# Two more units transposed by DMA, w_out conversions moved out of the last chunk, and a blockwise end

## The chip, the cores and the metric

The kernel runs on one core of one Trainium2 chip. The metric is the time of one execution on the device in microseconds (us); where several runs are given, their median. A core has five engines with a queue of instructions each: TensorE (PE; its weight loads are shown apart as PEld), VectorE (DVE), ScalarE (ACT), GpSimd (POOL) and SyncE (SP). SyncE only issues transfers here; 16 DMA engines carry them out. TensorE writes only to PSUM, whose contents VectorE or ScalarE have to take out ("evict") before the bank can be used again.

## The reference

A recurrent retention layer is followed by a feed-forward layer with SiLU. Cut to what matters:

```python
# q, k, v: (batch 4, heads 8, seq 768, head_dim 64), float32
gamma = 1.0 - 2.0 ** (-5.0 - np.arange(H, dtype=np.float32))
for t in range(S):
    state = gamma[None, :, None, None] * state + np.einsum('bhd,bhe->bhde', k[:, :, t], v[:, :, t])
    y[:, :, t] = scale * np.einsum('bhd,bhde->bhe', q[:, :, t], state)

x = y.transpose(0, 2, 1, 3).reshape(B * S, H * D)      # (3072, 512)
h = x @ w_in                                           # w_in (512, 2048)
g = h * (1.0 / (1.0 + np.exp(-h)))
out = g @ w_out                                        # w_out (2048, 512)
```

The two weights arrive as 64-bit floats (two 32-bit words per number), and the result is float32.

## The kernel before

The sequence is cut into 6 chunks of 128 positions. A unit is one chunk of one batch entry, so there are 24 units, numbered 0 to 23, four to a chunk. For each unit a "visit" m does three things for three neighbouring units: it prepares unit m, computes the scores and states of unit m - 1, and the output y of unit m - 2. Between the visits stand the products x @ w_in: 16 slices f of each chunk c, each of twelve 128x512 matmuls. Every float32 operand is split into a high and a low part and a mixed third one, so that one product is three matmuls: two add up in `ha` (or `oa`), one in `hb` (or `ob`), and an eviction combines the two. The results g go to DRAM and come back for the last part, g @ w_out.

A unit needs k and q with the head dimension on the partitions. Up to unit 16 TensorE transposes them (`stage_t`), from unit 17 on the DMA does: GpSimd pulls the 32-bit numbers apart into two 16-bit planes, the DMA transposes the planes, ScalarE puts them together.

```python
    FAR = 4 * B + 1                  # B = 4: from unit 17 on by DMA

    def part_t(n):
        for name, (p, tag, bufs) in (("q", (ld, "kf", 3)), ("k", (one, "kt", 2))):
            src = kqv[name].pop(n) if name == "q" else kqv[name][n]
            t = p.tile([128, 2 * H * D], U16, tag=tag, name=f"{name}p_{n}", bufs=bufs)
            nc.gpsimd.tensor_copy(out=t.rearrange("p (w h d) -> p w h d", w=2, h=H),
                                  in_=src.bitcast(U16).rearrange("p h (d w) -> p w h d", w=2))
            planes[name, n] = t

    def turn_t(n):
        for name, (p, tag, bufs) in (("q", (ld, "qf", 2)), ("k", (one, "qt", 3))):
            t = p.tile([128, 2 * HP, C], U16, tag=tag, name=f"{name}w_{n}", bufs=bufs)
            nc.sync.dma_start_transpose(out=t, in_=planes.pop((name, n)))
            turned[name, n] = t

    def join_t(name, n):
        ...
        nc.scalar.copy(out=to[n].bitcast(U16).rearrange("p a (t w) -> p w a t", w=2),
                       in_=turned.pop((name, n)).rearrange("p (w a) t -> p w a t", w=2))

    def stage_t(n):                  # up to unit 16
        for name, to, bufs, src, tp in (
                ("kt", kt, 2, kqv["k"][n], turn(f"kp_{n}")),
                ("qt", qt, 3, kqv["q"].pop(n), banks("q", f"qp_{n}", 1)[:, 0])):
            tp = tp.rearrange("p (a t) -> p a t", a=HP)
            for a in range(HP):      # HP = 4
                nc.tensor.transpose(tp[:, a, :], src[:, 2 * a : 2 * a + 2, :], ident)
            to[n] = one.tile([128, HP, C], FP32, tag=name, name=f"{name}_{n}", bufs=bufs)
            evac[:] = [nc.scalar.copy(out=to[n], in_=tp).ins]
```

A slice of a weight comes as 64-bit numbers. `convert_w` makes 32-bit ones with one ScalarE and five or six VectorE operations, with scratch tiles `ca`, `cs` and `cp`. `take_w` does this for the next slice; a w_out slice then goes to DRAM as 32-bit numbers, is read back in the last chunk and split there (`w_out`).

```python
        a = conv.tile([128, DM], U32, tag="ca", name=f"ca_{i}")
        s = conv.tile([128, DM], U32, tag="cs", name=f"cs_{i}")
        p = conv.tile([128, DM], U32, tag="cp", name=f"cp_{i}")
        ...
            nc.scalar.activation(out=a.bitcast(FP32), in_=hi.bitcast(FP32), func=AF.Abs, scale=65536.0)
        ...
        nc.vector.scalar_tensor_tensor(out=s, in0=a, scalar=3, in1=s,
                                       op0=ALU.logical_shift_left, op1=ALU.bitwise_or)
        nc.vector.tensor_scalar(out=p, in0=s, scalar1=0xFF800000, scalar2=None, op0=ALU.bitwise_and)
        nc.vector.scalar_tensor_tensor(out=p.bitcast(FP32), in0=lo, scalar=2.0 ** -52,
                                       in1=p.bitcast(FP32), op0=ALU.mult, op1=ALU.mult)
        # later: w = s + p
```

One product and its eviction; `turn` rotates through three PSUM banks:

```python
    def product_in(c, f):
        ha, hb = turn(f"ha_{c}_{f}"), turn(f"hb_{c}_{f}")
        for i in range(3):
            for kk in range(KIN):    # KIN = 4
                nc.tensor.matmul(hb if i == 2 else ha, lhsT=w_sb[f][:, i, ts(kk, 128)],
                                 rhs=xt[c][:, i, kk, :], start=kk == 0 and i != 1,
                                 stop=kk == KIN - 1 and i != 0)
        hs = hpool.tile([128, NT], FP32, tag="hs", name=f"g_{c}_{f}")
        copied[:] = [nc.scalar.activation(out=hs, in_=ha, func=AF.Copy, scale=ONE_E).ins]
        ...                          # joins of a unit follow here on ScalarE
        taken_out[:] = [nc.vector.tensor_tensor(out=hs, in0=hs, in1=hb, op=ALU.subtract).ins]
        ...                          # deferred VectorE work follows here
        nc.scalar.activation(out=hs, in_=hs, func=AF.Silu)
```

Which products a visit follows and which a conversion (NF = 16, `half` = 8; visit 14 follows the first entry of `at`):

```python
    takes += [(0, NF - 2), (2, half), (2, half + 2), (2, half + 4)]
    takes += [(3, f) for f in (0, 3, 7, 11, 14)]
    takes += [(4, f) for f in (3, 7, 11, 14)]
    takes += [(5, f) for f in (1, 3, 5)]
    ...
    at = ([(1, NF - 1)] + [(2, f) for f in range(NF - 7, NF - 2, 2)] +
          [(c, 4 * i + 1) for c in range(3, NC - 1) for i in range(B)])
```

In the last part every chunk has four blocks b, each with an `oa` and an `ob`. `split` splits the g that was read back.

```python
        for f in range(NF):
            n = c * NF + f
            split(n + S_AHEAD)
            ...
            for b in range(B):
                gh, glo, gm = (t[:, i, ts(b, C)] for i in range(3))
                oa, ob = acc[b]
                todo = [(oa, gh, 0), (oa, glo, 1), (ob, gm, 2)]

                for o, g, i in todo if c < NC - 1 else todo[2:] + todo[:2]:
                    nc.tensor.matmul(o, lhsT=g, rhs=wo[f][:, i, :], ...)
        for b in range(B):
            ...
            if c < NC - 1:
                nc.scalar.activation(out=o, in_=oa, func=AF.Copy, scale=ONE_E)
                nc.vector.tensor_tensor(out=o, in0=o, in1=ob, op=ALU.subtract)
                nc.scalar.dma_start(out=out[rows, :], in_=o)
                continue
            nc.scalar.copy(out=o, in_=ob)
            n = 2 if b == B - 1 else 1
            for i in range(n):       # o = ONE_E * oa - o, then the store from SyncE
                ...
```

Of the kernel before, what the change touches and what calls it, by code (L numbers as in the profile page):

```python
# [33 lines left out]
def kernel(  # L34
# [96 lines left out]
    kqv = {"k": {}, "q": {}, "v": {}}  # L131
    EARLY = 2 * B

    FAR = 4 * B + 1
    early = {}

    def load(name, n):
        if n >= len(units):
            return
        c, b = units[n]  # L140
        src = {"k": k, "q": q, "v": v}[name]
        if n < EARLY:

            if n not in early:
                early[n] = wpool.tile([128, 3, H, D], FP32, tag=f"w{4 + n}", name=f"kqv_{n}")
            t = early[n][:, "kqv".index(name)]
        else:
            t = ld.tile([128, H, D], FP32, tag=f"{name}f", name=f"{name}f_{n}",
                        bufs=2 if name == "q" else 3)
        nc.sync.dma_start(out=t, in_=src[b, :, ds(c * C, C)].rearrange("h t d -> t h d"))  # L150
        kqv[name][n] = t

# [24 lines left out]
    def convert_w(i):  # L177

        if i + W_AHEAD not in staged and i != 1:
            load_w(i + W_AHEAD)
        t = staged.pop(i)
        if not wide:  # L190
            return lambda: t
        words = t.rearrange("p (c w) -> p c w", w=2)
        lo, hi = words[:, :, 0], words[:, :, 1]
        a = conv.tile([128, DM], U32, tag="ca", name=f"ca_{i}")
        s = conv.tile([128, DM], U32, tag="cs", name=f"cs_{i}")
        p = conv.tile([128, DM], U32, tag="cp", name=f"cp_{i}")
        with tc.issue_after(evac[0]) if evac else ExitStack():
            nc.scalar.activation(out=a.bitcast(FP32), in_=hi.bitcast(FP32), func=AF.Abs,  # L198
                                 scale=65536.0)
# [9 lines left out]
        nc.vector.scalar_tensor_tensor(out=p.bitcast(FP32), in0=lo, scalar=2.0 ** -52,  # L209
                                       in1=p.bitcast(FP32), op0=ALU.mult, op1=ALU.mult)  # L210

        def rounded():
            w = (s.bitcast(FP32) if i < NF else
                 conv.tile([128, DM], FP32, tag="wl", name=f"cw_{i}"))
            nc.vector.tensor_tensor(out=w, in0=s.bitcast(FP32), in1=p.bitcast(FP32), op=ALU.add)
            return w

        return rounded
# [154 lines left out]

    def part_t(n):

        for name, (p, tag, bufs) in (("q", (ld, "kf", 3)), ("k", (one, "kt", 2))):
            src = kqv[name].pop(n) if name == "q" else kqv[name][n]
            t = p.tile([128, 2 * H * D], U16, tag=tag, name=f"{name}p_{n}", bufs=bufs)
            nc.gpsimd.tensor_copy(out=t.rearrange("p (w h d) -> p w h d", w=2, h=H),
                                  in_=src.bitcast(U16).rearrange("p h (d w) -> p w h d", w=2))  # L380
            planes[name, n] = t
# [162 lines left out]
    def halves(m):  # L544

        first, mid, last = (0 <= m - i < len(units) for i in range(3))
        if first and m < FAR:
            stage_t(m)
        if last:
            scores, states_with, yp = stage_y(m - 2)  # L550
            scores()
            states_with(0)
        yield
        if mid:
            sc, sums = score_tile(m - 1)
            stage_s(m - 1, sums)
            stage_a(m - 1, sc)
            if 1 < m <= 3 * B + 1 and units[m - 1][1] == 0:
                next_chunk()

            with tc.issue_after(taken_out[0]) if m > 3 * B + 1 else ExitStack():
                finish_a(m - 1, sc, sums)
            scale_q(m - 1)
            if m > 3 * B + 1 and units[m - 1][1] == B - 1:

                behind_copy.append(next_chunk)
        if m == 0:
            chunk_decays()
            first_chunk()
        if first and m < FAR:  # L570
            scale_k(m)
        if last:
            states_with(1)
            finish_y(m - 2, yp)

        if FAR <= m < len(units):
            with tc.issue_after(fenced[0]):
                part_t(m)
        for name in "kqv":
            for n in (m + 1, m + 2):  # L580
                if n >= EARLY and n == (m + 1 if name == "v" or n > FAR else m + 2):
                    load(name, n)
        if EARLY - 3 <= m < 3 * B + 2:
            with tc.issue_after(masked[0]):
                end_w()
                if m not in (EARLY - 2, EARLY):
                    begin_w()
# [32 lines left out]
    def get(n):  # L620
        if n >= len(order):
            return
        c, f = order[n]
        name = "kvqkvkqv"[n % 8]
        g = ld.tile([128, NT], FP32, tag=f"{name}f", name=f"gr_{c}_{f}",
                    bufs=2 if name == "q" else 3)
        nc.sync.dma_start(out=g, in_=g_dram[c, f])
        got[n] = g

# [73 lines left out]
    for i, x in enumerate(at):  # L703
# [35 lines left out]
    for c in range(NC):  # L739
        acc = []  # L740
        for b in range(B):
            if b < 2:
                u = banks("sy"[b], f"o{b}_{c}")
                acc.append([u[:, i] for i in range(2)])
            else:
                acc.append([turn(f"oa{b}_{c}"), turn(f"ob{b}_{c}") if b == 2 else
                            banks("q", f"ob{b}_{c}", 1)[:, 0]])
        for f in range(NF):
            n = c * NF + f
            split(n + S_AHEAD)  # L750
            if n < 4:
                w_out(NF - 4 + n)
            t = ready.pop(n)
            first_, last = f == 0, f == NF - 1
            for b in range(B):
                gh, glo, gm = (t[:, i, ts(b, C)] for i in range(3))
                oa, ob = acc[b]
                todo = [(oa, gh, 0), (oa, glo, 1), (ob, gm, 2)]

                for o, g, i in todo if c < NC - 1 else todo[2:] + todo[:2]:  # L760
                    nc.tensor.matmul(o, lhsT=g, rhs=wo[f][:, i, :], start=first_ and i != 1,  # L761
                                     stop=last and i != 0)
        for b in range(B):
            oa, ob = acc[b]
            o = one.tile([128, DM], FP32, tag=("kt", "qt")[b % 2], name=f"o_{c}_{b}",
                         bufs=(2, 3)[b % 2])
            rows = ds(b * S + c * C, C)
# [8 lines that stand above are left out]
            for i in range(n):  # L776
                cols = ts(i, DM // n)
                nc.vector.scalar_tensor_tensor(out=o[:, cols], in0=oa[:, cols], scalar=ONE_E,
                                               in1=o[:, cols], op0=ALU.mult,
                                               op1=ALU.subtract)  # L780
                nc.sync.dma_start(out=out[rows, cols], in_=o[:, cols])
# [30 lines left out]
```

## Time and profile before

Three runs took 628.95, 626.85 and 629.14 us; the median is 628.95. The profiled execution spans 625.6 us. By stretches (us from the start; busy time of each engine, and the busy share of the DMA engines):

| Stretch | What runs | PE | DVE | ACT | DMA share |
|---|---|---|---|---|---|
| 0 to 40 | loads, first units | 28.55 | 25.75 | 27.12 | 1.01 |
| 40 to 65 | units, first products | 21.64 | 21.42 | 21.85 | 0.90 |
| 65 to 103 | units among products | 37.00 | 36.10 | 33.28 | 0.85 |
| 103 to 175 | products of chunks 0 to 2 | 72.00 | 58.22 | 46.42 | 0.52 |
| 175 to 207 | units 14 to 17, rest of chunk 2 | 32.00 | 28.83 | 18.23 | 0.71 |
| 207 to 259 | chunk 3 | 52.00 | 39.08 | 34.25 | 0.99 |
| 259 to 311 | chunk 4 | 51.70 | 34.81 | 31.95 | 0.87 |
| 311 to 358 | chunk 5 | 46.57 | 39.73 | 32.74 | 0.64 |
| 358 to 577 | g @ w_out, chunks 0 to 4 | 219.00 | 120.30 | 64.37 | 0.39 (mean) |
| 577 to 621 | g @ w_out, chunk 5 | 43.57 | 17.11 | 9.18 | 0.14 |
| 621 to 626 | end | 0.00 | 1.17 | 0.16 | 0.58 |

The table is read by rows: an engine that is busy for as long as the stretch lasts sets its length. A busy share of the DMA engines near 1 means that transfers queue. The chain of work that ended last is followed back from the last instruction; what does not lie on it does not set the time.

### The profile page before, as it was taken

How to read it: one execution, taken by the hardware profiler on the slowest of the kernel's cores; microseconds unless marked ns; L12 is line 12 of the kernel's file. 1: busy time of each engine (PE TensorE's matmuls, PEld its weight loads, DVE VectorE, ACT ScalarE, POOL GpSimd, SP SyncE). 2: the span in 40 equal slices, each digit the busy share in tenths (PEclk: the TensorE clock that was granted, in tenths of full speed). 3: DMA queues.
4: the chain of work that ended last, by engine and by line, in shares of the span. 5: the costliest groups of instructions: out<-in, count | busy, mean ns of one | idle time of the engine just before them, and what ended most of it. 6: DMA issues, size and time to landing. Idle time of an engine off the chain costs nothing.

```text
span 625.6 us, 13502 instructions
## 1 busy us (share of the span) xinstructions
PE 604.0 (97%) x5384; PEld 497.1 (79%) x5384; DVE 422.5 (68%) x729; ACT 319.5 (51%) x611; POOL 22.5 (4%) x79
## 2 busy tenths in 40 slices
PE   5888999999999999999999999999999999999997
PEld 3777787888888888888787888888788888888885
DVE  2898998698889877766698795644635453644631
ACT  6688896666665556765566871412221221313211
POOL 3000000000000211111000000000000000000000
PEclk9899999999999999999999999999999999999999
DMA  9998886446558899989566673432524432433201
GB/s 201 205 216 205 230 222 200 166 151 200 206 161 233 246 244 239 253 225 264 198 236 204 205 228 104 150 119 85 179 74 131 140 102 101 148 122 110 93 1 68
DMA packets 137999, 107.32 MB, mean 172 GB/s; under 512 B 94800, under 2 KB 103248, under 8 KB 137936
## 3 DMA queue, kind: packets, MB, share of 16 engines
q1 hardware_dynamic: 135056, 101.21, 57.4%
q10 hardware_dynamic: 2880, 5.24, 2.3%
q8 instruction: 42, 0.69, 0.5%
q14 instruction: 21, 0.17, 0.1%
HBM read 66.06 MB, written 36.70 MB: 164 GB/s over the span
## 4 chain that ended last, share of the span: by engine, by line
PE 84%; DVE 5%; SPq 5%; DMA 2%; ACT 2%; issue 1%; DVEq 0%; ACTq 0%; POOLq 0%
PE ha L596 25%; PE o L761 21%; PE oa L761 14%; PE hb L596 12%; PE ob L761 7%; SPq L150 4%; PE y L462 3%; PE sc L419 1%; PE sc L429 1%; DMA wf<-in_moe_w_out_dram 1%; DMA wf<-in_moe_w_in_dram 1%; DMA kqv<-in_k_dram 1%; DVE g L604 1%; DVE xt L512 1%; DVE cs L205 1%
## 5 line engine op out<-in xcount | busy, mean ns | idle before, releaser
L596 PE MATMUL ha<-xt,wi 128*128 128x512 f32 x768 | 193.1, 393 | 1.1 <-DVE g L604 1.0
L596 PEld LDWEIGHTS ha<-xt,wi 128*128 128x128 f32 x768 | 142.1, 188 | 32.7 <-DVE g L604 2.3
L761 PE MATMUL o<-wo,gs 128*128 128x512 f32 x576 | 146.3, 389 | 0.0
L761 PEld LDWEIGHTS o<-wo,gs 128*128 128x128 f32 x576 | 108.1, 188 | 22.4
L653 DVE TENSOR_TENSOR gs<-gr,gs 128x512 fp32r<-128x512 f32 x96 | 62.3, 686 | 85.8 <-ACT gs L651 85.8
L651 ACT ACTIVATE gs<-gr 128x512 fp32r<-128x512 f32 x96 | 53.5, 621 | 128.3 <-issue 123.6
L761 PE MATMUL oa<-wo,gs 128*128 128x512 f32 x384 | 118.4, 389 | 0.0
L596 PE MATMUL hb<-xt,wi 128*128 128x512 f32 x384 | 102.9, 390 | 0.4 <-ACT g L600 0.4
L604 DVE TENSOR_TENSOR g<-g,hb 128x512 f32<-128x512 f32 x96 | 65.7, 684 | 45.6 <-ACT g L600 29.5
L596 PEld LDWEIGHTS hb<-xt,wi 128*128 128x128 f32 x384 | 71.9, 188 | 16.0 <-ACT g L600 1.1
L761 PEld LDWEIGHTS oa<-wo,gs 128*128 128x128 f32 x384 | 72.0, 188 | 15.3 <-ACT o L769 0.3
L608 ACT ACTIVATE g<-g 128x512 f32<-128x512 f32 x96 | 60.6, 631 | 43.7 <-DVE g L604 43.3
L761 PE MATMUL ob<-wo,gs 128*128 128x512 f32 x192 | 75.3, 392 | 0.3 <-DVE o L770 0.3
L600 ACT ACTIVATE g<-ha 128x512 f32<-128x512 f32 x96 | 56.9, 592 | 29.7 <-PE ha L596 22.1
L654 DVE SCALAR_TENSOR_TENSOR gs<-gs 128x512 fp32r<-128x512 f32 x96 | 62.3, 684 | 0.1
L761 PEld LDWEIGHTS ob<-wo,gs 128*128 128x128 f32 x192 | 36.0, 188 | 9.4 <-DVE o L770 2.1
L198 ACT ACTIVATE ca<-wf 128x512 f32<-128x512 f32 x32 | 21.6, 674 | 10.4 <-DVE cs L205 5.6
L209 DVE SCALAR_TENSOR_TENSOR cp<-wf,cp 128x512 f32<-128x512 uint32 x32 | 22.8, 712 | 0.6
L769 ACT ACTIVATE o<-o 128x512 f32<-128x512 f32 x10 | 6.0, 600 | 33.4 <-PE o L761 33.0
L205 DVE SCALAR_TENSOR_TENSOR cs<-ca,cs 128x512 uint32<-128x512 uint32 x32 | 22.1, 691 | 0.8
L462 PE MATMUL y<-qt,mid 64*64 64x64 f32 x384 | 20.6, 222 | 0.0
L770 DVE TENSOR_TENSOR o<-o,o 128x512 f32<-128x512 f32 x10 | 6.8, 688 | 19.3 <-ACT o L769 19.3
(85 smaller groups left out, 568.5 us busy)
## 6 DMA issues: line engine op xcount, KB each, us to landing
gd<-g SPq DMA_DIRECT2D x96, 256.0 KB, 3.1
gr<-gd SPq DMA_DIRECT2D x96, 256.0 KB, 2.7
wf<-in_moe_w_out_dram SPq DMA_DIRECT2D x16, 512.0 KB, 4.6
out_dram<-o ACTq DMA_DIRECT2D x20, 256.0 KB, 2.1
wf<-in_moe_w_in_dram SPq DMA_DIRECT2D x16, 256.0 KB, 3.8
wf<-in_moe_w_in_dram SPq DMA_DIRECT2D x32, 128.0 KB, 3.9
kf<-in_k_dram SPq DMA_DIRECT2D x16, 256.0 KB, 5.1
qf<-in_q_dram SPq DMA_DIRECT2D x16, 256.0 KB, 3.7
```

The lines of the kernel that those rows point to most:

```text
L150: nc.sync.dma_start(out=t, in_=src[b, :, ds(c * C, C)].rearrange("h t d -> t h d"))
L205: nc.vector.scalar_tensor_tensor(out=s, in0=a, scalar=3, in1=s, op0=ALU.logical_shift_left, op1=ALU.bitwise_or)
L209: nc.vector.scalar_tensor_tensor(out=p.bitcast(FP32), in0=lo, scalar=2.0 ** -52, in1=p.bitcast(FP32), op0=ALU.mult, op1=ALU.mult)
L462: i = nc.tensor.matmul(yp[ts(e, D), o, a, :], lhsT=lhsT, rhs=rhs, start=(e, o) not in started, stop=True, skip_group_check=True).ins
L596: nc.tensor.matmul(hb if i == 2 else ha, lhsT=w_sb[f][:, i, ts(kk, 128)], rhs=xt[c][:, i, kk, :], start=kk == 0 and i != 1, stop=kk == KIN ...
L600: copied[:] = [nc.scalar.activation(out=hs, in_=ha, func=AF.Copy, scale=ONE_E).ins]
L604: taken_out[:] = [nc.vector.tensor_tensor(out=hs, in0=hs, in1=hb, op=ALU.subtract).ins]
L608: nc.scalar.activation(out=hs, in_=hs, func=AF.Silu)
L651: nc.scalar.activation(out=t[:, 0, :], in_=g, func=AF.Copy, scale=HALF)
L653: nc.vector.tensor_tensor(out=t[:, 1, :], in0=g, in1=high, op=ALU.subtract)
L654: nc.vector.scalar_tensor_tensor(out=t[:, 2, :], in0=t[:, 1, :].bitcast(FP32), scalar=-1.0 / EPS, in1=high, op0=ALU.mult, op1=ALU.add)
L761: nc.tensor.matmul(o, lhsT=g, rhs=wo[f][:, i, :], start=first_ and i != 1, stop=last and i != 0)
```

## The change

It has three parts. First, units 15 and 16 are transposed by the DMA as well (FAR = 15). Their planes are made one visit earlier than the later units', and their loads keep the earlier schedule (SOON = 17). The tag of the k loads, which also holds the planes of q, gets a fourth buffer; the space comes from `cp`, which now is `ca`. Second, the conversions of w_out that were left for the last chunk are done in chunks 3 and 4, which takes them out of the stretch where the slices are also read back. Third, in the last chunk of g @ w_out all slices but two run in the order of the other chunks, and the last two block by block, so that a block is complete well before the next.

```diff
-    FAR = 4 * B + 1
+    FAR = 3 * B + 3
+    SOON = 4 * B + 1
+    LD_BUFS = {"k": 4, "q": 2, "v": 3}
...
-                        bufs=2 if name == "q" else 3)
+                        bufs=LD_BUFS[name])
...
-        p = conv.tile([128, DM], U32, tag="cp", name=f"cp_{i}")
+        p = a
...
-        for name, (p, tag, bufs) in (("q", (ld, "kf", 3)), ("k", (one, "kt", 2))):
+        for name, (p, tag, bufs) in (("q", (ld, "kf", LD_BUFS["k"])), ("k", (one, "kt", 2))):
...
-        if FAR <= m < len(units):
+        n = m if m >= SOON else m + 1
+        if FAR <= n < len(units) and (n < SOON or m >= SOON):
             with tc.issue_after(fenced[0]):
-                part_t(m)
+                part_t(n)
         for name in "kqv":
             for n in (m + 1, m + 2):
-                if n >= EARLY and n == (m + 1 if name == "v" or n > FAR else m + 2):
+                if n >= EARLY and n == (m + 1 if name == "v" or n > SOON else m + 2):
                     load(name, n)
...
-    takes += [(3, f) for f in (0, 3, 7, 11, 14)]
-    takes += [(4, f) for f in (3, 7, 11, 14)]
-    takes += [(5, f) for f in (1, 3, 5)]
+    takes += [(c, f) for c in (3, 4) for f in (0, 3, 6, 8, 11, 14)]
...
-    far = {steps.index(x): EARLY + 6 + i for i, x in enumerate(at)
-           if FAR <= EARLY + 6 + i < len(units)}
+    far = {steps.index(at[n - EARLY - 6 - (n < SOON)]): n for n in range(FAR, len(units))}
...
+        early_f = NF if c < NC - 1 else NF - 2
         for f in range(NF):
...
+            if f >= early_f:
+                continue
             for b in range(B):
...
-                todo = [(oa, gh, 0), (oa, glo, 1), (ob, gm, 2)]
-
-                for o, g, i in todo if c < NC - 1 else todo[2:] + todo[:2]:
+                for o, g, i in (oa, gh, 0), (oa, glo, 1), (ob, gm, 2):
...
+        for b in range(B if early_f < NF else 0):
+            oa, ob = acc[b]
+            for o, parts in (ob, (2,)), (oa, (0, 1)):
+                for f in range(early_f, NF):
+                    for i in parts:
+                        nc.tensor.matmul(o, lhsT=ready[c * NF + f][:, i, ts(b, C)],
+                                         rhs=wo[f][:, i, :], start=False,
+                                         stop=f == NF - 1 and i != 0)
```

More of the change, by code (lines that the diff above doesn't have):

```diff
@@ L625, in get @@
         g = ld.tile([128, NT], FP32, tag=f"{name}f", name=f"gr_{c}_{f}",
-                    bufs=2 if name == "q" else 3)
+                    bufs=LD_BUFS[name])
         nc.sync.dma_start(out=g, in_=g_dram[c, f])
@@ L752 @@
                 w_out(NF - 4 + n)
-            t = ready.pop(n)
-            first_, last = f == 0, f == NF - 1
+            t = ready[n]
+            if f >= early_f:
+                continue
             for b in range(B):
@@ L757 @@
                 oa, ob = acc[b]
-                todo = [(oa, gh, 0), (oa, glo, 1), (ob, gm, 2)]
-                for o, g, i in todo if c < NC - 1 else todo[2:] + todo[:2]:
-                    nc.tensor.matmul(o, lhsT=g, rhs=wo[f][:, i, :], start=first_ and i != 1,
-                                     stop=last and i != 0)
+                for o, g, i in (oa, gh, 0), (oa, glo, 1), (ob, gm, 2):
+                    nc.tensor.matmul(o, lhsT=g, rhs=wo[f][:, i, :], start=f == 0 and i != 1,
+                                     stop=f == NF - 1 and i != 0)
[6 more added lines that the diff above has]
+                                         rhs=wo[f][:, i, :], start=False,
+                                         stop=f == NF - 1 and i != 0)
         for b in range(B):
```

## The prediction

> **What bounds the kernel now.** I read the page first (busy times, the 40 slices), then the chain that ended last in order of time, then busy time by stretch, then the timeline of single engines where the chain leaves TensorE.
>
> ```profile
> PE 604.0 (97%) x5384; PEld 497.1 (79%) x5384; DVE 422.5 (68%) x729; ACT 319.5 (51%) x611; POOL 22.5 (4%) x79
> PE   5888999999999999999999999999999999999997
> DVE  2898998698889877766698795644635453644631
> DMA  9998886446558899989566673432524432433201
> PE 84%; DVE 5%; SPq 5%; DMA 2%; ACT 2%; issue 1%; DVEq 0%; ACTq 0%; POOLq 0%
> ```
>
> From the seventh slice (about 100 us) to the last, TensorE is busy without a break and is 84% of the chain. So from there on only three things can shorten the run: fewer TensorE instructions, the few gaps that are left, and the end after the last matmul. The change touches all three. The chain between 172 and 206 us shows one unit's visit with transposes on TensorE and, last, the first one without:
>
> ```profile
> 183.06 0.91 PE hb L596 x4
> 183.97 0.44 PE kp L403 x4
> 184.41 0.44 PE qp L403 x4
> 184.85 0.86 PE y L462 x48
> 186.87 2.04 PE ha L596 x8
> ...
> 200.20 0.91 PE hb L596 x4
> 201.10 0.86 PE y L462 x48
> 203.13 2.04 PE ha L596 x8
> ```
>
> Columns are start, duration, engine, tile, line, count. From the end of hb to the next ha takes 186.87 - 183.97 = 2.90 us with transposes, 203.13 - 201.10 = 2.03 us without: 0.87 us each. The gaps that are left, from the timelines:
>
> ```profile
> 339.09 0.66 ACT L198 ACTIVATE ca<-wf 128x512 f32<-128x512 f32 x1 [1.30 <-DMA wf<-in_moe_w_out_dram]
> 339.65 0.58 ACT L600 ACTIVATE g<-ha 128x512 f32<-128x512 f32 x1
> 340.28 1.20 PE L596 MATMUL hb<-xt,wi 128*128 128x512 f32 x4 [0.43 <-ACT g L600]
> ...
> 579.13 0.50 PE L761 MATMUL ob<-wo,gs 128*128 128x512 f32 x1 [0.35 <-DVE o L770]
> ...
> 620.25 2.75 SPq L781 DMA_DIRECT2D out_dram<-o  x5
> ```
>
> At 339 us ScalarE stands before the conversion of a w_out slice whose load has not landed, the eviction of ha behind it is late, and TensorE stops. At 579 us the last chunk begins with ob, whose bank VectorE frees last. At the end five output transfers are issued within 2.75 us.
>
> **What the Trainium skill says.** "SBUF — State Buffer", section "SBUF: two separate sides": VectorE and GpSimd share a port pair as an exclusive lock; a VectorE operation with two SBUF inputs and a GpSimd operation that reads SBUF block each other. The trace agrees: while unit 17's planes are split on GpSimd, two VectorE operations take 1.41 us that elsewhere take 0.69:
>
> ```profile
> 202.74 1.41 DVE L209 SCALAR_TENSOR_TENSOR cp<-wf,cp 128x512 f32<-128x512 uint32 x1
> 204.18 1.41 DVE L215 TENSOR_TENSOR cw<-cs,cp 128x512 f32<-128x512 f32 x1
> 202.34 1.25 POOL L379 COPY qp<-qf 128x1024 uint16<-128x1024 uint16 x1
> 203.54 1.51 POOL L379 COPY kp<-kf 128x1024 uint16<-128x1024 uint16 x1
> ```
>
> "DMA: Bandwidth & Descriptors", section "Issuing engines are not separate DMA queues": all transfers share the same 16 engines and interleave. So a transposing transfer competes with every load and store. The trace is full just there (columns: PE, PEld, DVE, ACT, POOL busy, clock, DMA share, GB/s):
>
> ```profile
> 235.00:251.00 16.00, 16.00 (x190) 13.23 (x189) 12.03 (x22) 10.78 (x19) 2.12 (x3) 1.00 1.09 240
> 299.00:311.00 12.00, 11.70 (x111) 9.42 (x110) 6.30 (x12) 6.08 (x11) 0.09 (x1) 1.00 0.61 215
> ```
>
> "DMA: Bandwidth & Descriptors", section "Anatomy of one DMA": a transfer has a fixed part of about 2 us, mostly completion. The output stores agree: 2.0 to 2.5 us from issue to landing.
>
> **The change part by part.**
>
> *Two more units by DMA.* The order of the built program loses exactly 16 TensorE transposes (4 for k and 4 for q, twice) in visits 15 and 16, and nothing else before the last chunk. 2 x 0.87 = 1.74 us off a path that is TensorE throughout. Added beside it: two GpSimd copies per unit (1.07 and 1.18 us mean), two transposing transfers (3.6 and 3.3 us to landing), and on ScalarE two joins of 1.36 us for two evictions of 0.58, that is 1.55 us more per unit. ScalarE has 9.93 busy of 17 us there (186 to 203 us), so it holds that. Data are there in time: unit 15's k and q are loaded two visits ahead, and between the transposing transfer and its join lies one more visit than for unit 17, whose join waited at most 1.2 us.
>
> *VectorE pays in that stretch.* It is nearly full: in the period 178.31 to 186.87 us 7.89 busy of 8.56, in the next 7.95 of 8.57. With the transposes gone a period is 7.69 us. The GpSimd copies will stand against about two two-input VectorE operations per visit, at 1.41 - 0.69 = 0.72 us each: 1.4 us a unit. So VectorE falls behind: 1.4 - 0.6 idle after visit 14, then 7.89 + 1.4 - 7.69 = 1.6, then 0.26: at worst about 2.7 us behind. The bank of an hb is written again two products later, after one product of 2.72 and one visit of 2.03: 4.75 us after it ends. The eviction takes 0.69, so VectorE may be nearly 4 us late before TensorE stops. I choose 0.3 us lost: net -1.4.
>
> *w_out slices.* 24 takes before and after. Three leave the last chunk's 16 products, one goes to chunk 3 and two to chunk 4. In the last chunk product starts lie 324.44 to 341.48 apart, 17.04 us for six periods of 2.72 (16.32): 0.72 lost; 341.48 to 347.22 is 5.74 for two: 0.30. With no conversion between the evictions both go: -1.0. Chunks 3 and 4 take about 3.4 us of VectorE per slice (0.42 + 0.42 + 0.69 + 0.43 + 0.71 + 0.75), where 10.7 to 12 of 16 us are busy; but 768 KB more per slice on DMA engines at a share of about 0.95. At 250 GB/s that is 3 us each, 9 us over about 100. I put +0.4 us for late transfers there.
>
> *The start of the last chunk.* oa now comes first, as in the other chunks. Their switches lose about 0.16 us (2.88 us against 2.72, at 401.62, 489.31 and 533.03); the last one 571.30 to 580.09, 8.79 for three periods of 8.16: 0.63. So -0.47.
>
> *The end.* Matmuls are the same in number. TensorE ends at 620.93, VectorE at 622.17, the DMA engines run at 380 GB/s from 621.2 to 624.0: 1 MB in one queue. With the last two slices block by block a block ends every 6 x 0.227 = 1.36 us instead of 0.68, so three of four stores are out before TensorE ends. What stays behind TensorE is two half evictions (0.4 us each), the issue and one transfer. I estimate 3.7 to 3.9 us instead of 4.67: -0.9.
>
> *One scratch tile fewer in the conversion* (cp is ca). ScalarE's next Abs then waits for the last addition rather than for L205. The built order puts it behind the ha eviction in three visits around 62 to 95 us, where the eviction stood up to 0.87 us behind that wait, and TensorE then 0.29. I take -0.2.
>
> Sum: -1.4 - 1.0 + 0.4 - 0.47 - 0.9 - 0.2 = **-3.6 us**: 628.95 - 3.6 = **625.4 us**, a ratio of 0.994.
>
> **Rivals.** *VectorE becomes the bound in visits 14 to 17.* For it: 92% busy and the doubled durations above. Against it: the 4 us of room in the banks. It would give back most of the 1.7, time about 627. *The DMA engines become the bound.* For it: shares of 0.95 to 1.09 from 219 to 267 us; a join that waits for its transposed plane holds ScalarE, which evicts ha in order. Against it: TensorE shows no gap there now with waits up to 1.2 us. With 2 to 3 us later transfers at several joins TensorE would lose 1 to 3 us: 626.5 to 628.5. *The gaps in the last chunk are filled by another wait*, for instance the w_out slices read back, whose loads landed 0.15 to 0.44 us late even now: 0.5 us less gain, 626. *Everything holds and the start gains more*, as the early stretch is a chain through VectorE and w_in loads that a new order may shorten by 1 us: 624.
>
> **Range and chances.** The parts are small and known to about 0.5 us each; the three runs before spread over 2.3 us, with 625.6 in the profile. That gives 622.8 to 628.0. A change of 2% is 12.6 us, far above anything the parts can give or cost: faster by over 2% 0.01, within 2% 0.98, slower by over 2% 0.01.
>
> **What would show it.** Right: TensorE has 5368 instructions; visits 15 and 16 take 2.03 us; no gap of TensorE between 310 and 350 us; the switch to the last chunk loses under 0.2 us; from TensorE's end to the end of the span under 4 us. VectorE shows 1.4 us operations beside GpSimd at about 178 and 186 us, and lags, but names no wait of TensorE. Wrong: a wait of TensorE for VectorE's g or am between 178 and 212 us, waits of ScalarE for qw or kw over 2 us, or a lost period in chunks 3 and 4. The prediction fails if such waits add up to over 3 us, or if the first 100 us move.

## The result

| Kernel | Median (us) | Range (us), runs | Ratio to before, 95% interval |
|---|---|---|---|
| before | 629.04 | 626.85 to 630.11, 6 | |
| changed | 635.37 | 633.68 to 638.43, 6 | 1.011 (1.0085 to 1.0135) |

The change makes the kernel 1.1% slower, 6.3 us, where 3.6 us less was predicted. It lies 7.4 us above the upper end of the range.

### The profile page after: what moved, and what is told of

Read it like the earlier page. It is cut to its first block, busy times and chain, and to the rows that moved or that the text cites. A ratio compares the mean times of both kernels' runs of the same rounds, so it can differ in the third digit from the quotient of the medians.

```text
span 633.7 us, 13489 instructions
## 1 busy us (share of the span) xinstructions
PE 604.8 (95%) x5368; PEld 495.7 (78%) x5368; DVE 425.2 (67%) x729; ACT 319.7 (50%) x611; POOL 28.0 (4%) x83
## 4 chain that ended last, share of the span: by engine, by line
PE 77%; DMA 5%; DVE 5%; ACT 5%; SPq 4%; issue 3%; ACTq 1%; DVEq 0%; POOLq 0%
PE ha L599 21%; PE o L761 20%; PE oa L761 13%; PE hb L599 10%; PE ob L761 7%; SPq L152 3%; PE y L464 2%; DMA qw<-qp 2%; PE sc L431 1%; DMA wod<-cw 1%; PE sc L421 1%; ACT qt L395 1%; ACT kt L395 1%; DMA kqv<-in_q_dram 1%; DVE g L607 1%
## 5 line engine op out<-in xcount | busy, mean ns | idle before, releaser
L761 PE MATMUL o<-wo,gs 128*128 128x512 f32 x564 | 143.2, 389 | 0.0
L761 PEld LDWEIGHTS o<-wo,gs 128*128 128x128 f32 x564 | 105.9, 188 | 21.9
L761 PE MATMUL oa<-wo,gs 128*128 128x512 f32 x376 | 116.0, 390 | 2.0 <-ACT o L778 2.0
L761 PEld LDWEIGHTS oa<-wo,gs 128*128 128x128 f32 x376 | 70.4, 188 | 17.3 <-ACT o L778 2.8
L761 PE MATMUL ob<-wo,gs 128*128 128x512 f32 x188 | 73.7, 392 | 0.0
L603 ACT ACTIVATE g<-ha 128x512 f32<-128x512 f32 x96 | 56.7, 590 | 23.3 <-PE ha L599 11.3
L207 DVE SCALAR_TENSOR_TENSOR cs<-ca,cs 128x512 uint32<-128x512 uint32 x32 | 23.6, 736 | 0.9
L211 DVE SCALAR_TENSOR_TENSOR ca<-wf,ca 128x512 f32<-128x512 uint32 x32 | 22.1, 691 | 0.6
```

Source lines behind the costliest of these rows:

```text
L761: nc.tensor.matmul(o, lhsT=g, rhs=wo[f][:, i, :], start=f == 0 and i != 1, stop=f == NF - 1 and i != 0)
```

## The profile after

The page of the changed kernel: busy time, the 40 slices of the DMA engines, and the shares of the chain that ended last.

```profile
PE 604.8 (95%) x5368; PEld 495.7 (78%) x5368; DVE 425.2 (67%) x729; ACT 319.7 (50%) x611; POOL 28.0 (4%) x83
...
DMA  9996885546589999999766543342433423343201
PE 77%; DMA 5%; DVE 5%; ACT 5%; SPq 4%; issue 3%; ACTq 1%; DVEq 0%; POOLq 0%
```

TensorE has the 5368 instructions that were expected, but its share of the chain falls from 84% to 77%, and that of transfers rises from 2% to 5%. The slices are too coarse to show where. Busy time by stretch shows it (columns: PE, PEld, DVE, ACT, POOL, clock, DMA share, GB/s):

```profile
175.00:207.00 32.00, 30.54 (x610) 24.95 (x609) 30.11 (x50) 19.68 (x33) 7.87 (x10) 1.00 0.93 218
...
259.00:311.00 52.00, 50.11 (x622) 40.93 (x612) 40.18 (x71) 33.18 (x54) 6.98 (x10) 1.00 0.96 272
```

In these two, units 14 to 17 and chunk 4, TensorE is busy 30.54 us of 32 and 50.11 of 52, where it had 32.00 and 51.70, and the DMA share went from 0.71 to 0.93 and from 0.87 to 0.96. The chain there:

```profile
208.19 0.04 ACT ca L200
...
209.34 0.50 ACT g L603
...
210.07 6.97 DMA qw<-qp
...
217.06 1.38 ACT qt L395
218.44 1.19 ACT kt L395
...
219.68 0.69 PE sc L431 x32
```

Unit 17's transposing transfer takes 6.97 us, its two joins follow on ScalarE, and TensorE's scores (`sc`) wait for them. A wait of this kind was the prediction's rival 2. A second loss is in a part of the kernel that the change does not touch, the switch from output chunk 0 to 1. ScalarE's timeline there:

```profile
407.93 3.02 ACTq L780 DMA_DIRECT2D out_dram<-o  x3
411.00 0.60 ACT L778 ACTIVATE o<-oa 128x512 f32<-128x512 f32 x1 [2.71 <-DMA out_dram<-o]
```

Three stores were issued within 1.56 us in the kernel before (at 401.02); here it takes 3.02, the eviction behind them is late, and TensorE loses 1.4 us.

To see where the time went, I took the starts of the products and of the output chunks from the timelines of TensorE and subtracted those of the kernel before. The table gives what each stretch adds (us). (c,f) is the product of chunk c and slice f, and a column begins where the one before it ends. The visits are in two parts: (2,8) to (2,12) has visits 15 and 16, (2,12) to (3,9) the three after them. "Switches" runs from the first output chunk to the last, "end" from the last matmul.

| Profile | to (2,8) | to (2,12) | to (3,9) | to (4,15) | chunk 5 | switches | last chunk | end | sum |
|---|---|---|---|---|---|---|---|---|---|
| changed | +2.46 | -0.94 | +2.82 | +3.53 | -0.97 | +1.15 | +0.81 | -0.77 | +8.1 |
| before, a second time | -0.02 | 0.00 | 0.00 | -0.16 | -0.42 | +0.04 | 0.00 | -0.13 | -0.7 |
| e1_scratch | +1.76 | 0.00 | 0.00 | -0.16 | -1.01 | -0.28 | -0.02 | -0.26 | 0.0 |
| e3_units | +0.31 | -1.75 | +3.44 | -0.16 | +0.16 | +2.81 | +1.59 | -0.01 | +6.4 |
| e7_takes_tail | +2.78 | 0.00 | 0.00 | +2.01 | -0.54 | -0.25 | -0.45 | -1.01 | +2.5 |
| e10_after_pad | +1.11 | -0.94 | +2.69 | +3.76 | -1.01 | -0.29 | -0.48 | -0.76 | +4.1 |
| e14_units_pad | +1.53 | -1.75 | +4.64 | -0.16 | -0.25 | -0.28 | -0.02 | 0.00 | +3.7 |
| e8_early | +3.02 | -1.75 | 0.00 | -0.16 | +0.31 | +1.27 | +1.03 | -0.01 | +3.7 |
| e12_scratch_tail | -0.26 | 0.00 | 0.00 | -0.16 | -1.01 | -0.25 | -0.45 | -1.03 | -3.2 |

A profile is one execution, not the median: those of e8_early and e9_wl2, for example, were the fastest of their runs (631.06 us of 631.06 to 637.17, 629.55 of 629.55 to 635.67).

## The experiments

Theory 1, 2 and 3 of the first four expectations are the shared scratch tile, GpSimd's copies, and full DMA engines. Later expectations call the last two B and C, and add A (the w_out takes between the visits) and D (TensorE's instruction fetch).

### The parts one by one

**e1_scratch**, the kernel before with only

```diff
-        p = conv.tile([128, DM], U32, tag="cp", name=f"cp_{i}")
+        p = a
```

> The kernel before with one line changed: the scratch tile cp of the weight conversion is ca. Theory 1 (the shared scratch tile makes ScalarE's next Abs wait for the last addition of the conversion before, and the evictions of ha stand behind that Abs in ScalarE's queue): 2 to 4 us slower than before, with ScalarE waiting for the addition of line 215 several us in total in chunks 3 to 5. Theory 2 (GpSimd's copies for the two added units hold VectorE up) and theory 3 (the DMA engines are full in chunks 2 to 4): the time of before within 0.7 us, because nothing of theirs is in this kernel.

626.81 us, ratio 0.9973 (0.9961 to 0.9985). Sharing the tile costs nothing by itself and makes this kernel a little faster. Theory 1 falls.

**e2_own_k3**, the changed kernel with a tile of its own for `p` and three k buffers:

```diff
-    LD_BUFS = {"k": 4, "q": 2, "v": 3}
+    LD_BUFS = {"k": 3, "q": 2, "v": 3}
-        p = a
+        p = conv.tile([128, DM], U32, tag="cp", name=f"cp_{i}")
```

> The changed kernel with the scratch tile cp back as a tile of its own, and three k buffers instead of four, which pays for its space. Theory 1: the loss is gone, 2 to 4 us faster than before (625 to 627 us). Theories 2 and 3: still 4 to 7 us slower than before (633 to 636), visits 16 to 18 still losing over 3 us together against the visits before.

635.10 us, ratio 1.0109 (1.0078 to 1.0139), the changed kernel's ratio again. The tile and the fourth buffer together are not the loss.

**e3_units**, the kernel before with only units 15 and 16 by DMA:

```diff
-    FAR = 4 * B + 1
+    FAR = 3 * B + 3
+    SOON = 4 * B + 1
```

(and the lines that use them, with three k buffers and `p` a tile of its own).

> The kernel before with only units 15 and 16 given to the DMA; scratch tile, three k buffers, conversions and the end as before. Theory 1: 1.2 to 1.7 us faster than before. Theory 2: 1 to 4 us slower, with TensorE waiting at visits 16 to 18 behind late evictions. Theory 3: 0 to 2 us slower, with joins on ScalarE waiting over 2 us for a transposed plane.

632.96 us, ratio 1.0082 (1.0052 to 1.0112). The two visits are shorter by 0.88 us each, as predicted, and yet this part alone costs 0.8%. In its profile 3.4 us are lost just behind the visits, and 4.4 in the output part, which has no unit in it.

**e7_takes_tail**, the kernel before with the moved takes and the blockwise end:

```diff
-    takes += [(3, f) for f in (0, 3, 7, 11, 14)]
-    takes += [(4, f) for f in (3, 7, 11, 14)]
-    takes += [(5, f) for f in (1, 3, 5)]
+    takes += [(c, f) for c in (3, 4) for f in (0, 3, 6, 8, 11, 14)]
```

(and the end as in the changed kernel).

> The kernel before with only the conversions moved to chunks 3 and 4 and the last chunk's new order and blockwise end; 17 units by TensorE, own scratch tile, three k buffers. Theory 1: 2 us faster than before (the gap in chunk 5 and the end), with at most 0.4 us lost in chunks 3 and 4. Theory 3: chunks 3 and 4 lose 2 us or more to late transfers, so that the time is that of before or longer.

628.24 us, ratio 1.0001 (0.9987 to 1.0015). The last chunk gains 0.45 at its start and 1.0 at the end, and chunks 3 and 4 lose 2.0.

### The slow stores of the output part

What the kernels with a loss at the switches (changed, e2, e3) have in common are 16 TensorE transposes fewer. The page of the changed kernel has a queue of kind "instruction" with 42 packets and 0.69 MB, 16 KB each: one for every 256 of TensorE's 10,736 matmul and weight-load instructions. The Trainium skill, "Runtime: NRT & Kernel Launch", section "Instruction fetch mechanics", says the same, that an engine fetches blocks of 256 instructions (16 KiB) through a DMA queue of its own, and that crossing a block is mostly hidden. Where it meets a switch here it is not hidden, as the following shows. An output chunk has 384 such instructions, so a switch meets the same place in a block every second chunk. With 36 TensorE instructions fewer (16 transposes, their 16 weight loads, four semaphore instructions) the fetch falls on the switch. DMA queues of the changed kernel between 408 and 411 us (packets, MB, share of 16 engines):

```profile
q10 hardware_dynamic: 273, 0.50, 45.2%
q8 instruction: 1, 0.02, 3.3%
```

3.3% of 16 engines over 3 us is 1.6 us of one engine, for one packet, in the middle of the stores. In the kernel before, the same stretch (400.5 to 404.5) has no such packet. All profiles agree: 13 stores to `out_dram` took over 1 us to issue, in six of the 17 profiles, and ahead of each a 16 KB packet had started, 0.1 to 0.4 us before.

**e10_after_pad**, the changed kernel with 18 transposes of the identity, whose result nobody reads, at the start:

```diff
+    dummy = banks("q", "dummy", 1)[:, 0]
+    for _ in range(18):
+        nc.tensor.transpose(dummy[:, :128], ident, ident)
     for m in range(EARLY + 1):
```

> The changed kernel with 18 dummy transposes of the identity on TensorE at the very start, into a bank that the first units use afterwards. They bring TensorE's count of instructions back to that of the kernel before (36 less in the changed kernel with semaphore instructions). Theory D: TensorE fetches its instructions 256 at a time through the DMA engines, and with 36 instructions less the fetch falls at every second switch of an output chunk (fetches at 409.0 and 585.2 us beside store issues that take 1.80 and 1.63 us instead of 0.34); with the dummies the fetches move away, all 20 store issues take about 0.34 us, the switch from chunk 0 to 1 loses 1.4 us less and the last switch about 0.4: 633.5 us. Rival: the slow store issues come from the reads of g or from the shift of the DMA semaphores by four; then they stay, 635.4.

631.13 us, ratio 1.0052 (1.0034 to 1.0069). The stores to `out_dram` of the changed kernel (issue time in ns: least, median, longest):

```profile
L780 ACTq DMA_DIRECT2D out_dram<-o x20: 338/339/1804, 407.9 to 588.4; - x20
```

and of this one:

```profile
L783 ACTq DMA_DIRECT2D out_dram<-o x20: 338/338/373, 406.6 to 584.4; - x20
```

No slow store is left. The switches add -0.29 instead of +1.15, the last chunk -0.48 instead of +0.81: 2.7 us. More work on TensorE made the kernel faster, by moving a fetch. Theory D holds for this part. The ratio fell by more, from 1.011 to 1.0052 (3.6 us); the profile has a further 1.35 us in its start, which is not explained.

**e14_units_pad**, the units-alone kernel with the same 18 transposes.

> The units-alone kernel (ratio 1.0082) with the 18 dummies. Theory D: no store issue over 1 us in the output part, so that the 2.85 us lost at two switches and up to 1 us in the last chunk come back, while the 1.65 us net loss between products (2,10) and (3,3) stays: ratio 1.0025. If the count of instructions means nothing for this kernel, 1.008.

631.25 us, ratio 1.0044 (1.0028 to 1.0060), against 1.0082: the output part is clean again (-0.28 and -0.02 for +2.81 and +1.59). The loss behind the visits stays (+4.64 for +3.44).

**e11_before_pad**, the kernel before with 46 of these transposes (92 instructions), and **e18_before_pad_again**, the same kernel for a second profile.

> The kernel before with 46 dummy transposes of the identity on TensorE at the very start: 92 instructions more, which puts TensorE's fetches (every 256 instructions, an output chunk has 384) where they would be at the switches of chunks 1 and 3 instead of 6.7 us ahead of those of chunks 0, 2 and 4. Theory D: one or two of the store issues at those switches take 1.2 to 1.9 us, and each such switch loses 1.3 to 1.5 us of TensorE: 630.3 to 631.7. Rival: the count of instructions means nothing; 628.9, or later by what the dummies take at the start, before the first product.

> The kernel before with 46 dummies once more, for a second profile. Theory D, with chance: store issues of 1.2 to 1.9 us at the switches of chunks 1 or 3 are there this time, and the profile is 1.3 us or more longer than 629.7. If the profile is again 629.7 without a slow store, the 7 us between the timed runs and the profile have another cause, which stays open.

e11: 637.01 us, ratio 1.0133 (1.0102 to 1.0164), but its profile, the fastest of its runs, shows +4.15 at the start and no slow store. e18: 636.77 us, a start 2.6 us later than that of e11, and at the switch to the last chunk:

```profile
540.06 3.28 ACTq L774 DMA_DIRECT2D out_dram<-o  x3
543.39 0.60 ACT L772 ACTIVATE o<-oa 128x512 f32<-128x512 f32 x1 [2.91 <-DMA out_dram<-o]
```

A fetch packet lies in the same 3 us (540 to 543), and the kernel loses 1.7 us there. So a fetch near a switch hits the stores in some executions and not in others. The test is not clean, as 46 transposes take 7.3 us at the start and delay the first units. What the start adds beyond that, and why it differs by 2.6 us between two executions of one program, stays open.

**e15_before_again**, the kernel before unchanged.

> The kernel before once more, for a second profile of it. If the start differs between executions, its first 100 us are 1 to 2.5 us longer than in the first profile, as in most of the other kernels' profiles, and the gap of 1.0 us in chunk 5 (339 us) may be missing. From 100 us to the end, but for that gap, it agrees within 0.3 us. If instead the start is the same to 0.3 us, the differences at the start are the changes' doing.

626.65 us. The first 100 us agree to 0.06 us: the expectation was wrong there. But e1 and e12 have the same program up to the output part, and their starts differ by 2.0 us; e11 and e18 are one program, and differ by 2.6. So the start differs between executions, though not in these two profiles, and the +2.46 of the changed kernel is not ascribed to the change. The gap in chunk 5 is smaller by 0.42 us with nothing changed.

### What the two units run into

In e3_units the chain behind the visits begins with w_out's slices:

```profile
199.39 5.49 DMA wod<-cw
...
204.98 0.70 DVE cw L217
...
205.88 0.38 SPq L239
...
206.36 0.38 SPq L152
...
206.83 0.89 SPq L617
...
207.81 6.89 DMA qw<-qp
```

The store of one slice takes 5.49 us to land; the next slice's addition into `cw` waits for it; its store, a load and a store of g go out from SyncE's queue, and only then the transposing transfer of unit 17, which takes another 6.89 us.

**e8_early**, the units-alone kernel with the four takes around the visits ahead of them:

```diff
-    takes += [(0, NF - 2), (2, half), (2, half + 2), (2, half + 4)]
+    takes += [(0, NF - 4), (0, NF - 2), (1, NF - 4), (1, NF - 2)]
```

> The units-alone kernel (units 15 and 16 by DMA, everything else as before, 632.96 us) with its four takes of w_out slices between (0,14) and (2,12) moved to (0,12), (0,14), (1,12), (1,14), ahead of the visits. Theory A: between 180 and 210 us the w_out chain (load of a slice, conversion, store of the converted slice, with one buffer for it) runs no faster than the full DMA engines let it, and SyncE's queue, in order, holds the transposing transfers of unit 17 behind it; with the takes gone from there the shorter visits keep their gain, the stretch up to product (3,3) loses none of the 3.4 us it lost, and the time falls by about 3.4 us to 629.5. Theory B: GpSimd's copies hold up VectorE; the three visits have less VectorE work now, so part of it comes back, but 1.4 us operations stay; 631 to 632. Theory C: the two transposing transfers of each unit alone fill the DMA engines; joins still wait 2 us; 632 to 633. In all of them the 2.85 us lost at the switches of the output chunks stays, as nothing here touches it.

634.58 us, ratio 1.0106 (1.0074 to 1.0139). The total did not fall, but the profile answers the question: from (2,12) to (3,9) nothing is lost (3.44 before), and the visits keep their -1.75. ScalarE's wait for `qw` between 186 and 222 us is down from 1.7 us to 0.6:

```profile
ACT qt L395 <- DMA qw<-qp: 0.6, 1, 0.6
```

The takes now collide with the products ahead of the visits: the product after (1,14) starts 2.46 us late, behind VectorE. So behind the visits it is the units and the takes together that are too much. This run doesn't tell DMA and VectorE apart, as moving a take relieves both.

**e9_wl2**, the units-alone kernel with `p = a` and two buffers for `cw`:

```diff
-                 conv.tile([128, DM], FP32, tag="wl", name=f"cw_{i}"))
+                 conv.tile([128, DM], FP32, tag="wl", name=f"cw_{i}", bufs=2))
```

(the low part of a split, which shares the tag, likewise).

> The units-alone kernel with p = a, and with two buffers instead of one for the converted slice (the tile cw, which shares its space with the low part of a split). Theory A: in the profile of the units-alone kernel the addition into cw at 204.98 waits 1.43 us for the store of the slice before, and the transposing transfers of unit 17 are issued at 207.8 behind it; with a second buffer that wait is gone, the transfers are issued 1.5 to 3 us earlier, and of the 3.4 us lost before product (3,3) 1.5 to 2.5 come back: 630.5 to 631.5. Theory C: the DMA engines are full whatever the order, so the wait moves to the next load: 632 to 633. Theory B expects no change but the 1.7 us that p = a gave on the kernel before: 631 to 633.

633.44 us, ratio 1.0086 (1.0056 to 1.0115), the same as without. In the profile 0.7 us of the 3.44 come back. The transposing transfer is still issued at 206.7 and still takes 6.91 us. The wait for the buffer was a small part.

**e16_turn_sooner**, e14_units_pad with the transposing transfers of every unit directly behind its visit:

```diff
-        if n - 1 in far:
-            turn_t(far[n - 1])
+        if n in far:
+            turn_t(far[n])
```

> The units-alone kernel with 18 dummies (ratio 1.0044), and the two transposing transfers of each unit issued right behind its visit and not one product later, which puts them ahead of one store of g in SyncE's queue, behind the loads and the w_out transfers as before. If the queue's order is the cause, they are issued about 1 us sooner for unit 17, the join starts 1 us sooner, and the 2.0 us lost at (3,2) falls to about 1: ratio 1.0025. If the DMA engines are simply full, the issue is sooner and the landing is not: 1.0045.

639.44 us, ratio 1.017 (1.0138 to 1.0201). The landing of the `qw` transfers in e14_units_pad, and then in this kernel:

```profile
DMA to landing us min/median/max: 3.4/4.0/6.7
```

```profile
DMA to landing us min/median/max: 4.2/5.4/6.9
```

A transfer issued sooner, right behind the loads of k and v, takes longer, and SyncE cannot issue the stores of g meanwhile (the one for unit 19 occupies the queue for 4.29 us). Between 222 and 255 us ScalarE then waits for free g buffers, and TensorE for ScalarE:

```profile
ACT g L603 <- DMA gd<-g: 9.5, 3, 4.3
...
PE hb L599 <- ACT g L603: 3.9, 2, 2.5
```

Issuing sooner does not help. The DMA totals and the main queue, before and then e14_units_pad:

```profile
DMA packets 137999, 107.32 MB, mean 172 GB/s; under 512 B 94800, under 2 KB 103248, under 8 KB 137936
q1 hardware_dynamic: 135056, 101.21, 57.4%
```

```profile
DMA packets 142223, 108.37 MB, mean 172 GB/s; under 512 B 99024, under 2 KB 107472, under 8 KB 142160
q1 hardware_dynamic: 139280, 102.26, 58.7%
```

Four more transposing transfers are 4224 more packets, all under 512 B, 1056 each. The packets together took 0.587 x 629.3 - 0.574 x 625.6 = 10.3 us more, as time of all 16 engines. That is not what the four transfers need by themselves: about 4 of the 10.3 us are packets of 1 KB and more, which both kernels have in the same number. And packets that are under way together are each counted in full: the share goes to 1.34 in the lines below, so that a share near 1 alone does not show that transfers queue. In the kernel before, a stretch with loads of q, k and v alone, and one with packets of transposing transfers alone (columns: PE, PEld, DVE, ACT, POOL, clock, DMA share, GB/s):

```profile
5.00:8.00 3.00, 1.66 (x7) 1.08 (x7) 0.35 (x1) 2.43 (x13) 0.55 (x2) 1.00 1.34 218
249.60:250.50 0.90, 0.90 (x6) 0.74 (x5) 0.87 (x4) 0.45 (x2) 0.00 (x0) 1.00 1.27 280
```

At 280 GB/s, 256 KB are through in 0.9 us; two such transfers per unit would be 1.9 us of the 7.7 that a visit and its two products last. So the lateness is not their own length, and it fits what is under way with them: in e3 the packets that start in the first 2.2 us of unit 17's transfer make 327 GB/s.

```profile
207.80:210.00 2.20, 1.87 (x9) 1.52 (x9) 2.17 (x5) 1.12 (x2) 0.00 (x0) 1.00 1.00 327
```

A part of the lateness is probably the fetch again. In the changed kernel a 16 KB packet starts at 214.81, within unit 17's transfer, and between 215.4 and 216.7 hardly a packet starts on any queue:

```profile
DMA packets 38, 0.01 MB, mean 7 GB/s; under 512 B 38, under 2 KB 38, under 8 KB 38
```

Seventeen packets of the transfer take 1.3 to 1.5 us each there and end together. In the 17 profiles, `qw` transfers with a fetch in their first 3 us took 4.84 us on average (24 of them), those with none near them 3.87 (85); for `kw` it is 4.52 (32) and 3.29 (97). It cannot be the whole loss: in e13 below no fetch lies in unit 17's transfer (4.27 us), and 1.2 us are lost behind it all the same.

**e13_all_eased** puts together: the units, `p = a`, three k and two `cw` buffers, the blockwise end, the 18 transposes, takes in chunks 3 to 5 as before, and two instead of three takes between the visits; **e17_all_sooner** adds the sooner issue.

```diff
-    takes += [(0, NF - 2), (2, half), (2, half + 2), (2, half + 4)]
+    takes += [(0, NF - 4), (0, NF - 2), (2, half), (2, half + 4)]
```

> Everything that the study found, put together: units 15 and 16 by DMA, the shared scratch tile, two buffers for the converted slice, one take of the four moved ahead of the visits so that two and not three stand between the visits (at (0,12), (0,14), (2,8), (2,12)), the later takes as in the kernel before, the blockwise end, and 18 dummy transposes at the start that keep TensorE's fetches where they were. If theories A and D name all of the loss: 3.1 us as in the kernel with scratch tile and end, and 1.74 for the transposes, less up to 1 us for the dummies at the start: 4 us less than the kernel before, ratio 0.9935. Rival C (the DMA engines are full with two units more): waits of joins remain and 1 to 3 us are lost between 175 and 222 us: 0.996 to 1.0.

> The kernel with everything together (ratio 1.0009) with the same sooner issue. If the queue's order is the cause, the 1.22 us lost at (3,2) and the 1.22 at (3,10) halve: ratio 0.999. If not, 1.001. In no case does it reach the kernel with scratch tile and end alone (0.9965) unless both losses go entirely.

e13: 628.27 us, ratio 1.0009 (0.9990 to 1.0028); e17: 636.27 us, 1.0106 (1.0077 to 1.0135). In e13 the visits and their followers add 0.39 + 1.29 us where 1.75 should have been gained, and chunks 3 and 4 another 1.22. Even eased, the units cost what the other parts bring. e17 loses 5.1 us in chunks 3 and 4, as e16 does (4.7).

### The version that beats both

**e12_scratch_tail**, the kernel before with `p = a` and the blockwise end, nothing else.

> The kernel before with only the shared scratch tile and the blockwise end: no unit more by DMA, no take moved, the same number of TensorE instructions. p = a alone measured a ratio of 0.9973; in the profile of the takes-and-end kernel the last chunk gained 0.45 us at its switch and 1.0 us behind the last matmul. If the parts are independent, 1.7 + 1.45 = 3.1 us less: a ratio of 0.995. Rival: the end's gain exists only in one profile and drowns in the variation of the start; 0.997.

625.97 us (623.91 to 628.65, 22 runs), ratio 0.9965 (0.9950 to 0.9979): 2.3 us less than the kernel before by the medians, with neither units nor takes moved, and 1.4% less than the changed kernel (0.9965 / 1.011).

## Why the prediction was wrong, step by step

**Two more units by DMA: the step that failed.** -1.74 on TensorE was right (-0.88 per visit in e3). "Data are there in time" was not. I took the transposing transfers at 3.6 and 3.3 us to landing, the medians of a kernel in which the longest took 6.0, and did not work out what else is under way where the new ones go; the two windows that I showed for full DMA engines lie behind that stretch, and one of them has a share of 0.61. In the changed kernel the `qw` of units 15, 16 and 17 landed after 5.03, 5.36 and 6.97 us. Visits and followers add +1.9 instead of -1.4. TensorE's timeline shows what it waits for:

```profile
194.86 0.69 PE L464 MATMUL y<-am,vf 64*64 64x64 f32 x32 [0.28 <-DVE xt L514]
202.96 0.69 PE L464 MATMUL y<-am,vf 64*64 64x64 f32 x32 [0.27 <-DVE xt L514]
205.10 0.69 PE L431 MATMUL sc<-qt,kt 64*64 64x64 f32 x32 [0.74 <-ACT kt L395]
219.68 0.69 PE L431 MATMUL sc<-qt,kt 64*64 64x64 f32 x32 [1.20 <-ACT kt L395]
```

The last two are scores that wait for the joins of units 16 and 17. With the takes of w_out moved away, nothing is lost behind the visits (e8), so the collision with these slices is a condition of that loss; the fetch in unit 17's transfer is probably a part of it. How the 3.3 us divide among slices, fetch and VectorE stays open. I had seen rival 2 and spoken against it because "TensorE shows no gap there now"; but that was the state before the transfers were added.

**VectorE.** The long operations beside GpSimd are there as predicted (1.53 us at 181.53, 1.28 at 187.60, 1.52 at 188.81, copies at 179.95 to 182.5 and 187.57 to 189.8), and VectorE is busy 30.11 of 32 us. TensorE names no wait for `g` or `am` there, but it does name VectorE: its `y` waits twice for `xt` (L514), 0.55 us in sum, and of the two visits only visit 15 keeps its 0.88 us. The chain of the changed kernel runs through VectorE and ScalarE from 182.8 us to unit 17's transfer. "Names no wait of TensorE" was thus wrong as well, and rival 1 is in part true.

**w_out slices.** Chunk 5 gives -0.97, as predicted, but partly by another cause than the one named: e1 and e12 give -1.01 with every take in its old place, and the second profile of before -0.42. Chunks 3 and 4 are mis-sized: +0.4 was the term, +2.0 is what the moved takes cost in e7 (with the end, which acts only later), and +3.53 in the changed kernel; why it is more there was not tested. In e7 the loss has the same shape, a late w_out load, then a transposing transfer of 4.24 us, a join, and scores that wait.

**Start of the last chunk.** -0.45 in e7, -0.48 in e10 against -0.47 predicted; in the changed kernel it became +0.81, by a fetch beside the stores (1.63 us for one of them at 585.4).

**The end.** -0.77 for -0.9; from the last matmul's end to the end of the span 3.9 us. (The DMA engines moved 359 GB/s at the end of the kernel before, from 621.2 to 624.0, not 380.)

**Scratch tile.** -0.2 was too small: e1 measured 0.27%, 1.7 us. ScalarE does wait for the addition, 5.8 us in sum between 186 and 222 us of the changed kernel, but e2, with a tile of its own for `p`, is no faster. Where e1 gains its 1.7 us is not shown: its profile has 1.01 less in chunk 5, but 1.76 more at the start.

**Missing from the sum: TensorE's fetches**, +2.7 us by e10. No term and no rival had them; removing instructions was taken as a gain only.

**"The first 100 us move"**: they did (+2.46), but the runs don't show that the change moves them.

In sum: units 3.3 us worse than predicted, chunks 3 and 4 3.1, switches and last chunk 2.4, the start 2.5, which makes 11.3 of the 11.7 us between -3.6 and the +8.1 of the profile.

## What to carry to other kernels

Before work moves from an engine to the DMA, list what is already under way in the very stretch where the transfers will go, in the same queue and on the same engines, and reckon with their longest time to landing on record and not with the median. A rival that has nothing against it but "there is no gap now" must be worked out with the added load. And where a switch without slack has stores or loads in it, look at the profile's instruction queue there: a changed number of instructions can move a fetch onto it, and a few dummy instructions in an idle place can move it away.

## What the runs showed of the hardware that I had not expected

- One instruction fetch of TensorE (16 KB) beside a store of 256 KB: the issue of that store takes 1.2 to 2.0 us instead of 0.34, and the three stores in a row at 408 us land after 4.2 us (median) instead of 2.1. The switches with one such store lost 0.8 to 1.7 us of TensorE, not hidden.
- A transposing transfer with such a fetch in its first 3 us landed about 1.0 to 1.2 us later than one without (means of 56 and 182 transfers in 17 profiles).
- Transposing transfers in 16-bit words, with no other packets beside theirs, moved 280 GB/s; plain loads of q, k and v in packets of the same size (256 bytes) moved 218, and the plain stores at the end, most of their bytes in packets of 2 KB, 359. The Trainium skill, "Advanced Engine Details and Errata", section "X-Bar Transpose (TRN2)", says that transposes are as fast as regular transfers and expects 350 to 400 GB/s; in this kernel the rate is lower, and the measurement decides.
